# Masks on ScalarE without GpSimd's three small operations, and the first chunk's reciprocals spread by matmuls instead of copies and transposes

## The chip, the core and the metric

The kernel runs on one core of a Trainium2 chip. The metric is the device time of one execution in microseconds (us). Engines are named as in the profile: PE is TensorE (PEld its weight loads), DVE is VectorE, ACT is ScalarE, POOL is GpSimd, SP is SyncE, which issues the DMAs.

## What is computed

Attention over 4 batches of 8 heads, 576 rows, head size 64, in which each row keeps only its 32 largest scores; behind it two MLPs of 512 to 2048 to 512 over the 2304 rows.

```
scores = scale * q @ k.T
kth = 32nd largest score of the row
scores = where(scores >= kth, scores, -1e9); attn = softmax(scores)
x = attn @ v                                   # (2304, 512)
h = x @ w_in;  x = (h - tanh(h)) @ w_out       # first MLP
h = x @ w_in;  out = elu(h) @ w_out            # second MLP
```

## The kernel before

**Tiling.** The 2304 rows are cut into six chunks of 384 rows (CHUNKS). A chunk has four pairs of heads, a pair two groups, a group three tiles of 128 rows by 576 scores: 48 groups of three tiles in all, eight per chunk. Chunk 0's attention has nothing beside it but the preparation of the weights (a 64-bit format that `prepare` turns into two float parts: ACT at L186, L203 and L148, DVE at L189, POOL at L149). From then on the MLP steps of one chunk run on PE beside the attention of the next chunk, whose search for the 32 largest scores runs on DVE.

**The search.** `topk_steps` (L387) makes a chain of four rounds for each group. A round has a `find` for each tile (DVE's MAX8, the eight largest values left, into the tile `vm`) and a `drop` for each tile. In rounds 0 to 2 `drop` is DVE's MATCH_REPLACE8 (L420), which takes the eight values out of the working copy. In round 3 the eighth value of `vm` is the row's 32nd largest score, the threshold, and `drop` makes the masked exponentials `e`, in one of two ways. For the first `by_act` tiles of a group ACT does it with two activations over 128x576: a Prelu (L422) that sends everything below the threshold to a very large negative number and leaves the rest, then an Exp (L423) that also sums the row. The other tiles have had their Exp in round 1 (L410), and DVE multiplies them by the comparison with the threshold (L427, a scalar_tensor_tensor that reads `s` and `e`). MASK_ACT sets `by_act`: three tiles per group in chunk 0 (not in its last group, which is the hurried one), two in chunk 1, one in chunk 2, none later. These are 7, 8 and 8 groups, 23 in all.

ACT's two activations need two small columns per tile: `nk`, minus the threshold, as the bias of the Prelu, and `b2`, the threshold times SCALE plus `mb`, as the bias of the Exp (`mb` is minus SCALE times the row's largest score, from round 0). POOL makes them in three operations on 128x3, 128x2 or 128x1 (L412, L413, L414), after the last of the group's MAX8 that ACT's tiles need. POOL's queue also holds the low parts of all operands (L149: gate, keys, weights), the low part of the queries (L326), the clearing of halves of the query tiles (L294), `mb` (L408) and the row sums (L498).

**Norm and attend.** `transposed` (L433) turns `e` round with PE transposes (L448) and copies it to `ph` on ACT (L449). `norm` (L490) takes the reciprocals of the row sums (DVE, L501, a tile `r` of 128x6) and has to spread them from "one per row" to a tile `rs` of 128x384, in which the 64 partitions of a head hold that head's reciprocals along the columns. For units with one head, as in chunk 0, ACT copies each reciprocal 64 times into `rw` (L513, one copy of 128x192 for each head), PE transposes `rw` in three pieces (L519), and ACT copies the result to `rs` (L532). For units with two heads, as in chunk 1, PE multiplies the column of `r`, repeated 64 times by a stride of zero as the weights, with the identity (L523); each such fp32 product is two MATMUL instructions. `attend` (L451) multiplies with the values (L470). The last pair of chunk 0 ("hurried") is the hand-over: its result is what the first MLP step waits for.

**The order.** The program issues all this in ticks (L731 on), but the framework's planner sets the order of each engine's queue from the order of issue, the priorities and its own estimate of each operation's time (`schedule_with_timeline_sim=True`, L809). On the chip each queue runs strictly in that order. `vm` and `b2` have two buffers each, so a group's `vm` is written again by the group after next, once every reader of the old content is done.

Of the kernel before, what the change touches and what calls it, by code (L numbers as in the profile page):

```python
# [8 lines left out]
F32 = mybir.dt.float32  # L9
# [4 lines left out]
AF = mybir.ActivationFunctionType  # L14
ALU = mybir.AluOpType
# [3 lines left out]
P = 128  # L19
# [4 lines left out]
SCALE = 0.125  # L24
# [3 lines left out]
NF = DFF // P  # L28
FILL = -1.0e38

STEEP = 3.0e38


CHUNKS = [
# [72 lines left out]
def tile_topk_attention_two_mlps(  # L107
# [9 lines left out]
    nc = tc.nc  # L117

    def pool(name, bufs, space=None):
        kw = {} if space is None else {"space": space}  # L120
        return ctx.enter_context(tc.tile_pool(name=name, bufs=bufs, **kw))

    const = pool("const", 1)
    sb = pool("sb", 2)
# [32 lines left out]
    def bank(tag, name, bufs):  # L157
        if tag == "h":
            if "park" in pairs:
                turns.close()  # L160
                del pairs["park"]
                pairs["h"] = pool("ph", 1, PSUM)
            return pairs["h"].tile([P, 512], F32, tag=tag, name=name, bufs=bufs)
        return ps.tile([P, 512], F32, tag=tag, name=name, bufs=bufs)
# [68 lines left out]
    for ci, size in enumerate(SIZES):  # L233
        for p in range(NPAIR):
            row = []
            c0 = 0
            for b, q0, n in CHUNKS[ci]:
                for heads in ([[0], [1]] if n >= 256 else [[0, 1]]):
                    u = Unit()
# [18 lines left out]
            for us in cuts:  # L258
                g = Group()
# [11 lines left out]
    def hurried(u):  # L271

        return u.rush and u.last
# [64 lines left out]
    def segments(u, t):  # L338

        out = []  # L340
        for i, h in enumerate(u.heads):
            lo, hi = max(0, i * u.n - t * P), min(P, (i + 1) * u.n - t * P)
            if lo < hi:
                out.append((lo, hi, h, t * P + lo - i * u.n))
        return out
# [41 lines left out]
    def topk_steps(g, r):  # L387

        k = len(g.tiles)
        if r == 0:  # L390
            g.vm = sb.tile([P, 4, 2, 8], F32, tag="vm", name=f"vm{g.id}")
            g.mb = sb.tile([P, 4], F32, tag="mb", name=f"mb{g.id}")
            g.sum = sb.tile([P, 4], F32, tag="sum", name=f"sum{g.id}", bufs=8)
            g.w = [sb.tile([P, S], F32, tag="w3", name=f"w3{g.id}_{j}", bufs=W_BUFS) for j in range(k)]
        if r == 1:
            for u in g.units:
                u.e = [sb.tile([P, S], F32, tag="e", name=f"e{u.id}_{t}", bufs=E_BUFS) for t in range(u.k)]

        by_act = 0 if g.rush and hurried(g.units[-1]) else min(k, MASK_ACT[g.units[0].ci])
        if r == 3 and by_act:  # L400
            g.nk = sb.tile([P, 4], F32, tag="nk", name=f"nk{g.id}")
            g.b2 = sb.tile([P, 4], F32, tag="b2", name=f"b2{g.id}")

        def find(j):
            u, t = g.tiles[j]
            nc.vector.max(g.vm[:, j, min(r, 1)], u.s[t] if r == 0 else g.w[j])  # L406
            if r == 0 and j == k - 1:
                nc.gpsimd.tensor_scalar_mul(g.mb[:, :k], g.vm[:, :k, 0, 0], -SCALE)  # L408
            if r == 1 and j >= by_act:
                nc.scalar.activation(u.e[t], u.s[t], AF.Exp, bias=g.mb[:, j : j + 1], scale=SCALE)  # L410
            if r == 3 and j == by_act - 1:
                nc.gpsimd.tensor_scalar_mul(g.nk[:, :by_act], g.vm[:, :by_act, 1, 7], -1.0)  # L412
                nc.gpsimd.tensor_scalar_mul(g.b2[:, :by_act], g.vm[:, :by_act, 1, 7], SCALE)  # L413
                nc.gpsimd.tensor_add(g.b2[:, :by_act], g.b2[:, :by_act], g.mb[:, :by_act])  # L414

        def drop(j):
            u, t = g.tiles[j]
            v = g.vm[:, j, min(r, 1)]
            if r < 3:
                nc.vector.match_replace(g.w[j], v, u.s[t] if r == 0 else g.w[j], FILL)  # L420
            elif j < by_act:
                nc.scalar.activation(u.e[t], u.s[t], AF.Prelu, bias=g.nk[:, j : j + 1], alpha=STEEP)  # L422
                nc.scalar.activation(  # L423
                    u.e[t], u.e[t], AF.Exp, bias=g.b2[:, j : j + 1], scale=SCALE, accum_out=g.sum[:, j : j + 1]
                )
            else:
                nc.vector.scalar_tensor_tensor(  # L427
                    u.e[t], u.s[t], v[:, 7:8], u.e[t], op0=ALU.is_ge, op1=ALU.mult, accum_out=g.sum[:, j : j + 1]
                )

        return [lambda j=j, d=d: d(j) for d in (find, drop) for j in range(k)]

    def transposed(g, blk):  # L433
# [52 lines left out]
    def spread(u):  # L486

        return u.ci >= 2 and not quick(u)

    def norm(ci, p, u):  # L490

        r = sb.tile([P, 8], F32, tag="r", name=f"r{ci}_{p}")
        a, seen = {}, {}
        at = 0
        for v in pair_units[ci, p]:
            if id(v.g) not in seen:
                seen[id(v.g)] = at
                nc.gpsimd.tensor_scalar_add(r[:, at : at + len(v.g.tiles)], v.g.sum[:, : len(v.g.tiles)], 1e-9)  # L498
                at += len(v.g.tiles)
            a[v.id] = seen[id(v.g)] + v.j0  # L500
        nc.vector.reciprocal(r[:, :at], r[:, :at])  # L501
        if spread(u):
            u.at = a
            u.flat = dr.tile([at * P], F32, tag=f"rd{ci}_{p}", name=f"rd{ci}_{p}")
            nc.sync.dma_start(u.flat.rearrange("(t p) -> p t", p=P), r[:, :at])
            return
        rt = bank("at", f"rt{ci}_{p}", 3)
        for v in pair_units[ci, p]:
            if len(v.heads) == 1:
                h = v.heads[0]  # L510
                if h == 0:
                    wide = sb.tile([P, 3, 2, D], F32, tag="rw", name=f"rw{v.id}", bufs=1)
                nc.scalar.activation(  # L513
                    wide[:, : v.k, h], r[:, a[v.id] : a[v.id] + v.k].unsqueeze(2).to_broadcast([P, v.k, D]), copy
                )
                if h == 1:
                    for t in range(v.k):
                        c = v.c0 + t * P
                        nc.tensor.transpose(rt[:, c : c + P], wide[:, t].rearrange("p h d -> p (h d)"), ident)  # L519
                continue  # L520
            for t in range(v.k):
                for lo, hi, h, c in segments(v, t):
                    nc.tensor.matmul(  # L523
                        rt[h * D : h * D + D, v.c0 + c : v.c0 + c + hi - lo],
                        r[:, a[v.id] + t : a[v.id] + t + 1].to_broadcast([P, D]),
                        ident[:, lo:hi],
                        start=True,
                        stop=True,
                    )
        n = SIZES[ci]  # L530
        u.rs = sb.tile([P, NMAX], F32, tag="rs", name=f"rs{ci}_{p}", bufs=1)
        nc.scalar.activation(u.rs[:, :n], rt[:, :n], copy)  # L532
# [198 lines left out]
    for tick in range(FIRST_TICK, n_ticks):  # L731
# [10 lines left out]
        for u in units:  # L742
            if hurried(u) and tick == 4 * u.g.at + 4:
                for blk in range(NB):
                    transposed(u.g, blk)
                norm(u.ci, u.p, u)
                attend(u)
                finish_pair(u)
        at, r = divmod(tick, 4)
        chain = topk_steps(groups[at], r) if 0 <= at < len(groups) else []  # L750
        todo = [step_parts(i) for i in at_tick.get(tick, ())]
        cuts = [len(chain) * j // (2 * max(1, len(todo))) for j in range(2 * max(1, len(todo)) + 1)]
# [60 lines left out]
```

## Time and profile before

| | us |
|---|---|
| median of 3 runs | 1217.75 (1216.57 to 1219.38) |
| the profiled execution | 1221.19 |
| its span, first to last instruction | 1219.4 |
| PE busy | 1150.4 (94%) |
| DVE busy | 950.1 (78%) |
| ACT busy | 764.1 (63%) |
| POOL busy | 503.1 (41%) |

The shares are over the whole span and mix stages. Cut into 40 slices, DVE is over 90% busy in nearly all of the first third and falls off later, PE is at 60 to 70% in the first five slices and at 90% or more from the eighth on, and ACT is full in slices three to six. The chain of work that ended last is PE almost alone (58% of the span, MATMULs of lines L613 and L577) back to 465 us, and DVE's search before that. So the first 465 us are where something other than PE can set the time.

### The profile page before, as it was taken

The page shows a single profiled execution, that of the slowest core. Times are in us where ns is not written, and L with a number is a line of the kernel's source. Part 1 is how long each engine was busy: PE and PEld are TensorE (multiplying, and loading weights), DVE is VectorE, ACT ScalarE, POOL GpSimd, SP SyncE. Part 2 cuts the span into 40 slices and gives each one's busy share as a digit, 9 for nine tenths or more (in the row PEclk, how much of TensorE's full clock was granted, in tenths as well). Part 3 has the DMA queues.
Part 4 walks back from the last instruction along what each step waited for, and adds up shares of the span by engine and source line. Part 5 has one row for each costly group of instructions (what it writes and reads, how often), then busy time and mean ns, then how long its engine had stood idle before and what let it go on. Part 6 is the DMA issues. An engine that isn't in the chain of part 4 may idle for free.

```text
span 1219.4 us, 18848 instructions
## 1 busy us (share of the span) xinstructions
PE 1150.4 (94%) x6349; PEld 976.2 (80%) x6349; DVE 950.1 (78%) x1896; ACT 764.1 (63%) x1592; POOL 503.1 (41%) x557
## 2 busy tenths in 40 slices
PE   6477789998999999999999999999999999999998
PEld 3344478887887978898988988988988988898897
DVE  7899999998999999789888779898789996100111
ACT  4999978988975546474564666575555564432333
POOL 2345348666752323253524444434434413333221
PEclk9688899998999999999999999999999999999999
DMA  7999728984989985759886779988679875686572
GB/s 233 361 354 336 241 73 295 365 288 142 385 345 290 288 302 144 246 162 315 251 187 206 238 239 247 226 243 271 218 248 221 205 154 207 210 285 247 195 270 95
DMA packets 81328, 299.59 MB, mean 246 GB/s; under 512 B 18768, under 2 KB 36048, under 8 KB 51664
## 3 DMA queue, kind: packets, MB, share of 16 engines
q1 hardware_dynamic: 81232, 298.39, 76.8%
q8 instruction: 50, 0.82, 0.3%
q14 instruction: 46, 0.38, 0.1%
HBM read 252.97 MB, written 45.39 MB: 245 GB/s over the span
## 4 chain that ended last, share of the span: by engine, by line
PE 58%; ACT 2%; DVE 1%; POOL 0%; issue 0%; ACTq 0%; POOLq 0%; DVEq 0%
PE acc L613 24%; PE h L577 24%; PE av L470 3%; PE pt L448 3%; PE ps L383 2%; PE ps L384 2%; DVE vm L406 0%; ACT y L627 0%; DVE w L420 0%; ACT zh L632 0%; ACT e L410 0%; ACT ph L449 0%; ACT s L385 0%; POOL kk L149 0%; ACT t L583 0%
## 5 line engine op out<-in xcount | busy, mean ns | idle before, releaser
L149 POOL TENSOR_TENSOR gl<-g,gh 128x384 fp32r<-128x384 f32 x192 | 203.4, 1061 | 371.8 <-ACT gh L148 352.3
L406 DVE MAX8 vm<-w 128x8 f32<-128x576 f32 x432 | 315.8, 748 | 3.2
L613 PE MATMUL acc<-wt,gh 128*128 128x512 f32 x1002 | 267.2, 398 | 0.3 <-ACT gh L148 0.3
L420 DVE MATCH_REPLACE8 w<-vm,w 128x576 f32<-128x576 f32 x288 | 212.8, 740 | 0.0
L613 PEld LDWEIGHTS acc<-wt,gh 128*128 128x128 f32 x1002 | 183.7, 188 | 33.9 <-issue 2.7
L148 ACT ACTIVATE gh<-g 128x384 fp32r<-128x384 f32 x192 | 100.6, 526 | 83.8 <-DVE g L591 43.3
L591 DVE SCALAR_TENSOR_TENSOR g<-t,h 128x384 f32<-128x384 f32 x96 | 52.4, 545 | 127.8 <-ACT t L583 127.4
L577 PE MATMUL h<-zh,wt 128*128 128x384 f32 (+2 forms) x768 | 145.8, 326 | 2.4 <-ACT zh L632 1.2
L613 PE MATMUL acc<-wt,gl 128*128 128x512 f32 x501 | 146.4, 398 | 0.0
L577 PE MATMUL h<-xh,wt 128*128 128x384 f32 x664 | 140.0, 339 | 2.0 <-DVE g L591 1.2
L448 PE MATMUL pt<-ident,e 128*116 128x128 f32 (+1 forms) x720 | 117.8, 290 | 20.2 <-ACT e L423 8.3
L385 ACT ACTIVATE s<-ps 128x288 f32<-128x288 f32 (+1 forms) x272 | 106.8, 416 | 45.2 <-PE ps L384 36.6
L406 DVE MAX8 vm<-s 128x8 f32<-128x576 f32 x144 | 107.4, 751 | 34.6 <-ACT s L385 32.6
L577 PEld LDWEIGHTS h<-zh,wt 128*128 128x128 f32 x768 | 124.9, 190 | 8.8 <-ACT zh L632 2.4
L449 ACT ACTIVATE ph<-pt 116x384 f32<-116x384 f32 (+1 forms) x240 | 111.2, 500 | 30.0 <-PE pt L448 29.5
L448 PEld LDWEIGHTS pt<-ident,e 128*116 128x116 f32 (+1 forms) x720 | 90.4, 143 | 43.2 <-ACT e L423 11.4
L577 PEld LDWEIGHTS h<-xh,wt 128*128 128x128 f32 x664 | 116.2, 188 | 9.0 <-DVE g L591 1.5
L582 ACT ACTIVATE t<-h 128x384 f32<-128x384 f32 x96 | 46.7, 488 | 108.2 <-PE h L577 108.0
L613 PEld LDWEIGHTS acc<-wt,gl 128*128 128x128 f32 x501 | 92.1, 188 | 18.5
L420 DVE MATCH_REPLACE8 w<-vm,s 128x576 f32<-128x576 f32 x144 | 106.6, 741 | 0.0
L580 ACT ACTIVATE t<-h 128x384 f32<-128x384 f32 x96 | 47.0, 491 | 90.9 <-PE h L577 90.8
L596 DVE TENSOR_TENSOR g<-h,t 128x384 f32<-128x384 f32 x76 | 41.4, 546 | 72.0 <-ACT t L580 71.5
(82 smaller groups left out, 1958.3 us busy)
## 6 DMA issues: line engine op xcount, KB each, us to landing
wt<-w SPq DMA_DIRECT2D x167, 1024.0 KB, 6.0
wr<-in_w_dram SPq DMA_DIRECT2D x32, 1024.0 KB, 8.9
w<-wp SPq DMA_DIRECT2D x32, 1024.0 KB, 8.4
kraw<-in_kT_dram SPq DMA_DIRECT2D x96, 144.0 KB, 5.4
vraw<-in_vL_dram SPq DMA_DIRECT2D x64, 160.0 KB, 5.2
sd<-sp SPq DMA_DIRECT2D x24, 288.0 KB, 5.8
s<-sd SPq DMA_DIRECT2D x24, 288.0 KB, 8.9
qraw<-in_qT_dram SPq DMA_DIRECT2D x64, 96.0 KB, 5.6
```

What stands on the lines that cost most here:

```text
L148: nc.scalar.activation(hi, src, copy)
L149: return nc.gpsimd.tensor_sub(lo, src, f(hi))
L385: nc.scalar.activation(s[lo:hi, cs], pt[lo:hi, :HS], copy)
L406: nc.vector.max(g.vm[:, j, min(r, 1)], u.s[t] if r == 0 else g.w[j])
L420: nc.vector.match_replace(g.w[j], v, u.s[t] if r == 0 else g.w[j], FILL)
L448: nc.tensor.transpose(pt[:kn, j * P : j * P + P], v.e[t][:, k0 : k0 + kn], ident)
L449: nc.scalar.activation(g.ph[:kn, blk, :nq], pt[:kn, :nq], copy)
L577: nc.tensor.matmul(h[:, cs], wv[:, wi, kt], xs[:, kt, cs], start=(a == 0), stop=(a == len(jobs) - 1))
L580: nc.scalar.activation(t, h, AF.Tanh)
L582: nc.scalar.activation(t, h, AF.Relu, scale=-1.0)
L591: nc.vector.scalar_tensor_tensor(g, t, -1.0, h, op0=ALU.add, op1=ALU.max)
L613: nc.tensor.matmul(acc[ci, m][t], gx[:, t * P : t * P + P], wt[:, wi], start=(ft == 0 and k == 0), stop=(ft == NF - 1 and k == 2),)
```

## The change

Two edits. The mask's first activation now takes minus the score plus the threshold (scale -1, bias the threshold itself out of `vm`), so that what is kept is negative or zero; the Prelu multiplies that part by 2^-100 and leaves the positive part, which is to vanish; the Exp's scale is -SCALE times 2^100. `nk` is gone, and `b2` is one scalar_tensor_tensor on DVE. In `norm`, chunk 0 takes the way of the units with two heads.

```diff
-STEEP = 3.0e38
+FLAT = 2.0**-100
...
         if r == 3 and by_act:
-            g.nk = sb.tile([P, 4], F32, tag="nk", name=f"nk{g.id}")
             g.b2 = sb.tile([P, 4], F32, tag="b2", name=f"b2{g.id}")
...
             if r == 3 and j == by_act - 1:
-                nc.gpsimd.tensor_scalar_mul(g.nk[:, :by_act], g.vm[:, :by_act, 1, 7], -1.0)
-                nc.gpsimd.tensor_scalar_mul(g.b2[:, :by_act], g.vm[:, :by_act, 1, 7], SCALE)
-                nc.gpsimd.tensor_add(g.b2[:, :by_act], g.b2[:, :by_act], g.mb[:, :by_act])
+                nc.vector.scalar_tensor_tensor(
+                    g.b2[:, :by_act], g.vm[:, :by_act, 1, 7], SCALE, g.mb[:, :by_act], op0=ALU.mult, op1=ALU.add
+                )
...
             elif j < by_act:
-                nc.scalar.activation(u.e[t], u.s[t], AF.Prelu, bias=g.nk[:, j : j + 1], alpha=STEEP)
+                nc.scalar.activation(u.e[t], u.s[t], AF.Prelu, bias=v[:, 7:8], scale=-1.0, alpha=FLAT)
                 nc.scalar.activation(
-                    u.e[t], u.e[t], AF.Exp, bias=g.b2[:, j : j + 1], scale=SCALE, accum_out=g.sum[:, j : j + 1]
+                    u.e[t], u.e[t], AF.Exp, bias=g.b2[:, j : j + 1], scale=-SCALE / FLAT, accum_out=g.sum[:, j : j + 1]
                 )
...
         for v in pair_units[ci, p]:
-            if len(v.heads) == 1:
+            if ci and len(v.heads) == 1:
                 h = v.heads[0]
```

In the last hunk chunk 0's four pairs leave out eight copies (L513) and twelve transposes (L519) and go on to the loop at L521 with six products each; the quick pairs of chunks 2, 3 and 5 keep the copies.

## Rows read from the trace of the kernel before

**Rows 1.** Busy time by stage: PE, PEld, DVE, ACT, POOL, then clock, DMA share, GB/s
```profile
34.00:165.00 131.00, 97.38 (x394) 61.13 (x394) 127.78 (x255) 122.83 (x244) 55.93 (x71) 0.80 0.83 294
165.00:330.00 165.00, 154.62 (x927) 135.12 (x927) 155.61 (x283) 142.62 (x279) 113.34 (x104) 0.97 0.75 272
330.00:465.00 135.00, 132.23 (x777) 110.35 (x773) 133.51 (x276) 80.60 (x162) 47.80 (x69) 1.00 0.90 289
```

**Rows 2.** Timeline of PE: start, duration, what, in brackets its idle time and releaser
```profile
174.16 2.29 PE L577 MATMUL h<-xh,wp 128*128 128x384 f32 x8 [2.69 <-DVE g L596]
...
200.33 0.40 PE L383 MATMUL ps<-kk,qs 128*128 128x288 f32 x1 [2.25 <-ACT s L385]
...
368.47 1.66 PE L577 MATMUL h<-xh,wt 128*128 128x384 f32 x8 [1.18 <-DVE g L591]
...
465.22 1.66 PE L577 MATMUL h<-zh,wt 128*128 128x384 f32 x8 [0.76 <-DVE g L591]
```

**Rows 3.** Line L412 on POOL (min/median/max ns), and its main wait (us, times)
```profile
L412 POOL TENSOR_SCALAR nk<-vm x23: 213/224/1202, 36.7 to 475.1; 128x2 f32<-128x2 f32 x8, 128x1 f32<-128x1 f32 x8, 128x3 f32<-128x3 f32 x7
...
  DVE vm L406: 21.5, 11
```

**Rows 4.** Timelines of DVE, POOL and ACT around 195 us
```profile
191.18 0.74 DVE L406 MAX8 vm<-w 128x8 f32<-128x576 f32 x1
...
192.64 2.31 POOL L149 TENSOR_TENSOR kk<-kraw,kk 128x576 fp32r<-128x576 f32 x1
194.93 0.21 POOL L412 TENSOR_SCALAR nk<-vm 128x2 f32<-128x2 f32 x1
...
195.18 1.45 ACT L422 ACTIVATE e<-s,nk 128x576 f32<-128x576 f32 x2 [3.18 <-POOL nk L412]
```

**Rows 5.** Timeline of DVE: a small operation, and an operation behind the one it reads
```profile
62.43 0.18 DVE L501 RECIPROCAL r<-r 128x6 f32<-128x6 f32 x1
62.53 2.04 DVE L406 MAX8 vm<-w 128x8 f32<-128x576 f32 x3
...
82.67 0.74 DVE L420 MATCH_REPLACE8 w<-vm,s 128x576 f32<-128x576 f32 x1
83.44 0.76 DVE L406 MAX8 vm<-w 128x8 f32<-128x576 f32 x1
```

**Rows 6.** L427 from 165 us on, by line and by group; one of them, and POOL beside it
```profile
L427 DVE SCALAR_TENSOR_TENSOR e<-s,vm,e x23: 793/808/1816, 176.5 to 477.0; 128x576 f32<-128x576 f32 x23
...
L427 DVE SCALAR_TENSOR_TENSOR e<-s,vm,e 128x576 f32<-128x576 f32 x22 | 22.3, 1014 | 0.2
...
196.82 1.50 DVE L427 SCALAR_TENSOR_TENSOR e<-s,vm,e 128x576 f32<-128x576 f32 x1
...
195.31 2.40 POOL L149 TENSOR_TENSOR wp<-wf,wp 128x1024 fp32r<-128x1024 f32 x1
```

**Rows 7.** Timelines of DVE and POOL around 119 us
```profile
117.39 1.41 DVE L406 MAX8 vm<-w 128x8 f32<-128x576 f32 x2
...
118.16 2.39 POOL L149 TENSOR_TENSOR wp<-wf,wp 128x1024 fp32r<-128x1024 f32 x1
...
120.92 1.23 DVE L189 SCALAR_TENSOR_TENSOR wf<-wr 128x1024 uint32<-128x1024 uint32 x1 [1.27 <-POOL b L413]
```

**Rows 8.** Timelines of ACT and PE: the spreading of the reciprocals, both ways
```profile
155.98 0.35 ACT L513 ACTIVATE rw<-r 128x192 f32<-128x192 f32 x1
156.23 0.48 ACT L449 ACTIVATE ph<-pt 116x384 f32<-116x384 f32 x1
...
159.09 0.55 PE L519 MATMUL rt<-ident,rw 128*128 128x128 f32 x3
...
214.96 0.94 PE L523 MATMUL rt<-ident,r 128*64 128x128 f32 x16
```

**Rows 9.** Timelines of ACT and DVE around 40 us: the readers and the next writer of vm
```profile
38.41 2.10 ACT L422 ACTIVATE e<-s,nk 128x576 f32<-128x576 f32 x3
...
39.78 0.75 DVE L406 MAX8 vm<-s 128x8 f32<-128x576 f32 x1
```

## The prediction

> **What bounds the kernel now.** I read the busy time by stage first, because a share over the whole span mixes stages with different limits. From 34 to 165 us DVE is busy 127.78 of 131 us and ACT 122.83, while PE has a quarter of the time free; from 165 to 330 us PE (154.62 of 165) and DVE (155.61) run level; from 330 to 465 us DVE has 1.5 us of 135 free and PE 2.8 [rows 1]. So the search on DVE sets the length of the first stage, and it paces the next two together with PE. Then I read PE's timeline for its idle time, since the chain that ended last is PE almost alone from 465 us on, so that every gap ahead of that is carried to the end. Four gaps matter: 2.69 us at the hand-over, 2.25 us at 200 us, 1.18 us at 368 us and 0.76 us at 465 us [rows 2]. Three are released by a gate on DVE, and the one at 200 us by an ACT copy. What makes that copy late is in the timelines just before it: ACT stood 3.18 us before a Prelu for POOL's `nk`, which started at 194.93 behind a split of the keys of 2.31 us, although the MAX8 that it needed had started at 191.18 [rows 4]. This is the place at which POOL in the mask's path costs time.
>
> **The change, part by part.**
>
> *What leaves POOL.* 69 operations of about 0.2 us, and L412's waits for DVE, 21.5 us in 11 cases [rows 3]. No gap of PE in [rows 2] is released by POOL, so this is worth nothing by itself. What is behind it on POOL's queue, the low parts of gates, keys and weights, comes earlier or stays.
>
> *What leaves ACT's wait.* The Prelu now waits for the MAX8 alone. At 195 us that takes away up to 3.18 us on ACT, and the copy, and PE's products behind it, move up. PE gets back at most its own gap: -2.25, which I take whole, since a gate of ACT and not of DVE was last there. Ends: -3.2, if what is queued behind the wait on ACT gains as well, and 0, if DVE is late by then. Other waits for `nk` are followed by no gap of PE that ACT released; I count them as nothing, covered by the products that PE has queued.
>
> *What comes to DVE: its own time.* 23 scalar_tensor_tensors on a few columns. No row has one; the nearest is the reciprocal of 128x6, which takes 0.18 us, but the next operation starts 0.10 us after it [rows 5]. Each stands right behind the MAX8 that it reads. Such a neighbour costs more: a MAX8 that reads what the operation before it wrote started 0.77 us after it, where two independent ones are 1.41 - 0.76 = 0.65 us apart [rows 5, 7], so 0.12 on top. I take 0.10 + 0.11 = 0.21 each; ends 0.08 (no dependence cost, and shorter than the reciprocal) and 0.30 (0.18 + 0.12). In chunk 0 there are 7, on the engine that sets the stage: +1.5 (0.6 to 2.1). In chunk 1 there are 8, +1.7 on DVE, which has 165 - 155.61 = 9.4 us free there: nothing, and +1.7 if the cover is gone. In chunk 2, 7 of the 8 lie before 465 us, with DVE full and two of PE's gaps waiting for it: +1.5 (0.6 to 2.1).
>
> *What comes to DVE: waiting beside POOL.* The new operation reads two tiles of SBUF, `vm` and `mb`. The nearest row of that kind is the masks by DVE, L427, which reads `s` and `e`: median 0.81 us, but mean 1.01 and maximum 1.82, and the one at 196.82 took 1.50 us while a POOL subtraction that had started at 195.31 ran until 197.71 [rows 6]. So such an operation can be held until POOL's is over. The mean addition is 1.01 - 0.81 = 0.20 us. For 7 in chunk 0 that is +1.4; one place can be seen: the MAX8s end at 118.80 while POOL's subtraction runs until 120.55, 1.75 us more, but DVE is idle for 1.27 us just behind [rows 7], which takes back most of it. With the 3.2 us that DVE has free in the stage [rows 1], I take half: +0.7 (0 to 2.2). In chunk 2 POOL had mostly stood waiting at these places, as the 11 waits show [rows 3], so I take 0 (up to 7 times 0.20 = 1.4).
> The Trainium skill's page "SBUF — State Buffer", section "Who interferes with whom", says that a DVE instruction with two SBUF inputs contends with a GpSimd instruction that reads SBUF, and that whoever comes first keeps the shared port for the whole instruction. By that rule the small operation is blocked for whatever is left of a POOL operation, so it speaks against the change, and the row at 196.82 agrees with it; by the mean it would put 23 times 0.20 = 4.6 us on DVE, where I count 0.7.
>
> *The reader of `vm`.* ACT's Prelus now read `vm` themselves, so the group after next can write it only when they are done. In group 0 they end at 40.51, and the next writer started at 39.78 [rows 9]: 0.73 us of wait for DVE in the old order. The planner knows of it and has other MAX8s to put first: 0 (up to 0.7).
>
> *The reciprocals.* Eight copies leave ACT; each held it for 156.23 - 155.98 = 0.25 us [rows 8]. Six of them lie in the stage that DVE sets, where ACT has 8 us free of 131 [rows 1] but now and then keeps DVE waiting for scores: 6 times 0.25 = 1.5 us of ACT, of which I take -0.6 (0 to -1.5). Two lie at the hand-over among the copies that the products with the values wait for: -0.5. Against that, twelve products replace three transposes in each pair. The 16 of a later pair took 0.94 us for as many columns (8 of 128 and 8 of 64, or 12 of 128), the three transposes 0.55 [rows 8]: +0.4 at the hand-over on PE, nothing in the other pairs, where PE is free. Together at the hand-over -0.1 (-0.5 to +0.4).
>
> **Sum:** 1.5 + 0.7 + 1.5 - 2.25 - 0.6 - 0.1 = +0.75, say +0.8 us. The profiled execution took 1221.19 us, 3.4 above the median of the runs, so 1222.0 in its terms and 1218.5 against the median of 1217.75. A measurement of this kernel can tell some 0.2% (2.4 us) from no change, so this is no change.
>
> **Rivals.** *Faster: ACT is the one that is relieved.* The whole wait of 3.18 us is won and not only PE's gap, all six copies count (-1.5), the hand-over gains its 0.5, and the new operations cost their low end (14 times 0.08 = 1.1): -3.18 - 1.5 - 0.5 + 1.1 = -4.1, or 1213.7 us. For it: ACT is 94% busy in the first stage and the only engine that was seen to wait long for `nk` [rows 1, 4]. Against: the gaps of PE at 368 and 465 us are DVE's [rows 2], and a faster ACT doesn't move those. A new order by the planner could add to it: the gate behind the 2.69 us at the hand-over [rows 2] stands among MAX8s, and if it is put earlier, part of that is won too.
>
> *Slower: the wait for the port decides.* Each new operation is held behind POOL's subtraction in progress, on the engine that sets the time. With the mean of 0.20 on top of 0.21 everywhere that is 14 times 0.41 = 5.7 us before 465 us; in chunk 1 8 times 0.41 = 3.3 us use up a third of DVE's free time, and if the gate that PE needs behind 200 us is then late, the 2.25 us aren't won: 5.7 - 0.7 = +5.0, or 1222.8 us; with the 2.25 won, 1220.5. It decides from about 0.4 us each on: 14 times 0.4 = 5.6 against gains of 3. For it: [rows 6] and DVE's share in [rows 1]. Against: at most of these places POOL was idle, and the first stage has some slack. The rule of the page named above is this rival's mechanism.
>
> *No net effect because both happen* is the forecast itself; the `vm` wait (+0.7) changes nothing in it.
>
> **How the numbers follow.** Forecast (within 0.2%): 0.38. Faster: 0.34; slower: 0.28. Gains and costs are of one size, each hangs on one row that shows it once, and the planner may lay out the order anew, so neither side gets less. The range takes in both rivals' times and a part of the hand-over's 2.69 at the low end: 1212.5 to 1223.0; the forecast's own is the 0.2% to either side of the median, 1215.3 to 1220.2. It leaves out about 1 in 10 on each side, a new order that costs or gains more.
>
> **What would show it.** Right: no ACT wait before a Prelu of more than a few tenths; PE's gap near 200 us gone; the new DVE line with a median under 0.3 us and a few of more than 0.5 where POOL subtracts; the products behind the hand-over's gap, at 174.16 before [rows 2], one to two us later. Wrong: the new line's mean above 0.5 us (slower); DVE's idle time before 330 us grown, or a hand-over that starts earlier (faster); or a gap of several us at a place where neither edit acts, which would be the planner's order.

## The result and the profile after

After the change the kernel takes 1225.95 us (median of 4 runs, 1223.43 to 1226.79); the kernel before, on the same chip, 1217.16 (4 runs, 1216.42 to 1219.38). The ratio is 1.0066, 95% interval 1.0045 to 1.0086: 8.8 us slower by the medians, outside the predicted range.

The stages of after, as in [rows 1]:

```profile
34.00:165.00 131.00, 98.52 (x429) 63.08 (x428) 128.75 (x261) 120.33 (x234) 49.97 (x50) 0.82 0.83 296
165.00:330.00 165.00, 156.09 (x942) 136.32 (x940) 159.63 (x295) 145.94 (x283) 107.42 (x82) 0.97 0.80 278
330.00:465.00 135.00, 129.26 (x731) 107.69 (x730) 132.00 (x281) 76.07 (x155) 42.14 (x47) 0.99 0.87 273
```

POOL is busy some 6 us less in each stage. DVE has 4 us more from 165 to 330 us, and from 330 to 465 us PE does 46 instructions fewer. PE's larger gaps in after (timeline of PE, to be laid beside [rows 2]):

```profile
172.69 1.65 PE L576 MATMUL h<-xh,wp 128*128 128x384 f32 x8 [1.13 <-DVE g L595]
...
195.34 2.93 PE L576 MATMUL h<-xh,wp 128*128 128x384 f32 x8 [2.69 <-DVE g L595]
...
277.79 0.89 PE L447 MATMUL pt<-ident,e 128*116 128x128 f32 x3 [2.80 <-ACT s L385]
...
334.32 0.54 PE L447 MATMUL pt<-ident,e 128*116 128x128 f32 x3 [2.92 <-ACT ph L448]
...
472.69 1.67 PE L576 MATMUL h<-zh,wt 128*128 128x384 f32 x8 [1.76 <-DVE g L590]
```

The gap at 200 us that ACT's copy released is gone, and there are others at 195, 334 and 472 us. The one at 277 us is not new. The kernel before has it too, released by ACT as well, and [rows 2] leaves it out (timeline of PE, before):

```profile
277.74 0.61 PE L383 MATMUL ps<-kk,qs 128*128 128x288 f32 x1 [2.28 <-ACT s L385]
```

What stands behind two of the others is seen on DVE, POOL and ACT of after (timelines; the lines are from 190 and from 333 us):

```profile
190.75 3.40 DVE L189 SCALAR_TENSOR_TENSOR wf<-wr 128x1024 uint32<-128x1024 uint32 x1
194.08 0.75 DVE L405 MAX8 vm<-w 128x8 f32<-128x576 f32 x1
194.75 0.53 DVE L595 TENSOR_TENSOR g<-h,t 128x384 f32<-128x384 f32 x1
...
190.69 2.39 POOL L149 TENSOR_TENSOR wp<-wf,wp 128x1024 fp32r<-128x1024 f32 x1
...
332.83 1.06 ACT L148 ACTIVATE wp<-wf 128x1024 fp32r<-128x1024 f32 x1 [1.24 <-DVE wf L189]
333.79 0.85 ACT L448 ACTIVATE ph<-pt 116x384 f32<-116x384 f32 x2
```

At 195 us the gate (L595) that PE waits for stands on DVE's queue behind the joining of a weight, which itself was held beside POOL until 193.08, and behind a MAX8. At 334 us the copy that PE waits for stands on ACT's queue behind a split that waits for DVE. Neither is an operation that the change added: it is what the planner put in front of what.

The new operation in after, by its line (count, then min/median/max ns):

```profile
L411 DVE SCALAR_TENSOR_TENSOR b<-vm,mb x23: 136/152/1495, 36.8 to 474.5; 128x2 f32<-128x2 f32 x8, 128x1 f32<-128x1 f32 x8, 128x3 f32<-128x3 f32 x7
```

The longest case, on DVE, and POOL beside it (timelines of after):

```profile
36.81 1.50 DVE L411 SCALAR_TENSOR_TENSOR b<-vm,mb 128x3 f32<-128x3 f32 x1
...
35.93 4.70 POOL L149 TENSOR_TENSOR wp<-wf,wp 128x1024 fp32r<-128x1024 f32 x2 [0.97 <-ACT wp L148]
```

Its median is 0.15 us, but the one at 36.81 took ten times that, while POOL ran subtractions that had begun 0.88 us earlier. So after shows both suspects at once: operations held beside POOL, and a new order with gaps where neither edit acts. The experiments take them apart.

### The profile page after: what moved, and what is told of

It is laid out like the page before. It is cut to its first block, busy times and chain, and to the rows that moved or that the text cites. A ratio compares the mean times of both kernels' runs of the same rounds, so it can differ in the third digit from the quotient of the medians.

```text
span 1224.9 us, 18889 instructions
## 1 busy us (share of the span) xinstructions
PE 1154.6 (94%) x6385; PEld 980.3 (80%) x6385; DVE 956.6 (78%) x1919; ACT 763.7 (62%) x1584; POOL 486.5 (40%) x488
## 4 chain that ended last, share of the span: by engine, by line
PE 66%; DVE 16%; ACT 8%; DMA 5%; issue 3%; POOL 1%; SPq 1%; ACTq 0%; POOLq 0%; DVEq 0%
PE h L576 27%; PE acc L612 26%; DVE vm L405 6%; DVE w L419 5%; PE av L469 4%; PE pt L447 4%; DMA wr<-in_w_dram 2%; PE ps L383 2%; PE ps L384 2%; DVE wf L189 1%; DVE e L426 1%; DMA s<-sd 1%; ACT s L385 1%; ACT wr L203 1%; DMA w<-wp 1%
## 5 line engine op out<-in xcount | busy, mean ns | idle before, releaser
L612 PE MATMUL acc<-wt,gh 128*128 128x512 f32 x1002 | 266.7, 398 | 0.5 <-ACT gh L148 0.5
L612 PEld LDWEIGHTS acc<-wt,gh 128*128 128x128 f32 x1002 | 183.6, 188 | 36.3 <-issue 3.9
L612 PE MATMUL acc<-wt,gl 128*128 128x512 f32 x501 | 146.9, 398 | 0.0
L447 PE MATMUL pt<-ident,e 128*116 128x128 f32 (+1 forms) x720 | 115.3, 286 | 26.1 <-ACT e L422 11.7
L612 PEld LDWEIGHTS acc<-wt,gl 128*128 128x128 f32 x501 | 92.2, 188 | 18.5
L595 DVE TENSOR_TENSOR g<-h,t 128x384 f32<-128x384 f32 x76 | 41.4, 545 | 71.5 <-ACT t L579 71.1
```

What stands on the lines that cost most here:

```text
L447: nc.tensor.transpose(pt[:kn, j * P : j * P + P], v.e[t][:, k0 : k0 + kn], ident)
L612: nc.tensor.matmul(acc[ci, m][t], gx[:, t * P : t * P + P], wt[:, wi], start=(ft == 0 and k == 0), stop=(ft == NF - 1 and k == 2),)
```

## The experiments

Theory A: the new operations on DVE, held beside POOL, make the loss. Theory B: the new order makes it. Theory C: the reciprocals' edit makes it.

### Each part alone, a variant, and a neutral edit, the order left to the planner

The mask edit alone, which is the diff without its last hunk:

> The mask edit alone; the first chunk's reciprocals are spread as before, and the planner lays the order out for this program. Theory A (the 23 new operations on DVE, held behind POOL, set the loss: about 9.8 us of DVE in the profile after, 6 of it where DVE sets the time): nearly the whole loss is here, ratio to before 1.004 to 1.008. Theory B (the planner's new order, the search ahead of the MLP's gates, makes the loss, and the operations cost little): an order of its own again, so the ratio is not tied to that of the whole change; anything from 0.996 to 1.008, with gaps of PE at other places than after's 195, 334 and 472 us. Theory C (the reciprocals by six matmuls make the loss): 0.998 to 1.001.

Measured: 1234.62 us against 1216.87, ratio 1.0148 (1.0130 to 1.0166). A part of the change loses twice what the whole loses, which is beyond the ranges of A and B alike.

The reciprocals' edit alone, which is that last hunk:

```
-            if len(v.heads) == 1:
+            if ci and len(v.heads) == 1:
```

> The reciprocals' edit alone; the masks are as before. Theory A: no more than its own small terms, -0.6 to +0.4 us, ratio 0.9985 to 1.0005. Theory B: the planner lays the order anew for this program as well, so the ratio can leave 0.998 to 1.002 on either side although only 8 copies and 12 products differ. Theory C: 1.004 to 1.008.

Measured: 1226.52 us, 1.0083 (1.0069 to 1.0097). The two parts' losses together would be 0.023, the whole has 0.0066: with the order left to the planner the parts don't add. B's range takes this in, and the interval does not rule out C's.

Both edits, with a bias that reads one tensor of SBUF:

```
-                nc.vector.scalar_tensor_tensor(
-                    g.b2[:, :by_act], g.vm[:, :by_act, 1, 7], SCALE, g.mb[:, :by_act], op0=ALU.mult, op1=ALU.add
-                )
+                for i in range(by_act):
+                    nc.vector.tensor_scalar(
+                        g.b2[:, i : i + 1], g.vm[:, i, 1, 7:8], SCALE, g.mb[:, i : i + 1], op0=ALU.mult, op1=ALU.add
+                    )
```

> Both edits, but the new bias is made by one tensor_scalar for each tile, with mb as its scalar, so that each reads one tensor of SBUF and does not share the port with POOL: 69 operations in place of 23. Theory A: their median stays at 0.06 to 0.15 us each and none is held for over 0.3 us, so 5 to 6 us of the loss are gone: ratio to before 0.999 to 1.002. Theory B: the holds go as well, but the time follows the order that the planner makes: anything from 0.996 to 1.008.

Measured: 1221.20 us, 1.0043 (1.0027 to 1.0059); there are 45 of the new operations, not the 69 that this expectation and a later one count. Theory A's 0.999 to 1.002 is missed, and B allows nearly anything, so by itself this run settles nothing.

The kernel before with two lines swapped:

```
-                nc.gpsimd.tensor_scalar_mul(g.nk[:, :by_act], g.vm[:, :by_act, 1, 7], -1.0)
                 nc.gpsimd.tensor_scalar_mul(g.b2[:, :by_act], g.vm[:, :by_act, 1, 7], SCALE)
+                nc.gpsimd.tensor_scalar_mul(g.nk[:, :by_act], g.vm[:, :by_act, 1, 7], -1.0)
```

> The kernel before with two of POOL's three small operations in the other order in the code (b2 is scaled before nk is made); the same instructions, the same work. Theory A and theory C: no difference, ratio 0.999 to 1.001. Theory B: the planner lays the order anew from there on, and the time moves by 2 us or more, ratio below 0.998 or above 1.002.

Measured: 1223.66 us, 1.0060 (1.0047 to 1.0073). The work is the same; `nk` comes one small POOL operation later, some 0.2 us [rows 3], and the planner lays out the order again. It costs 7 us, almost what the change costs. Since leaving `nk` out altogether wins only 1.7 us in the old order (below), the 0.2 us can hardly be the cause; the swap was not run with the old order held. Two of its gaps (timeline of PE):

```profile
175.21 0.52 PE L383 MATMUL ps<-kk,qs 128*128 128x288 f32 x1 [3.67 <-ACT s L385]
...
198.66 1.19 PE L613 MATMUL acc<-wp,gl 128*128 128x512 f32 x3 [1.84 <-POOL gl L149]
```

### The same edits with the old order held

To measure the edits without a new order, each engine's instructions were chained in the order that they have in the kernel before. At the end of the tile function stands

```
+    for _e, _perm in _ord.items():
+        _mine = [i for i in tc.nc.cur_bb.bb.instructions if str(i.engine) == "EngineType." + _e and type(i).__name__ != "BassTilePoolBoundary"]
+        for _a, _b in zip(_perm, _perm[1:]):
+            tc.add_manual_dep(_mine[_b], _mine[_a].name, mybir.DependencyInfo(mybir.DependencyClass.NoSync, mybir.DependencyReason.DATA), reason="pin")
```

with a table of the order. The chain is of the kind that asks for no semaphore (`NoSync`). In the profiles, the kernels held in this way run what they share with the kernel before in its sequence on PE, DVE, ACT and POOL, by operation, tile and shape; the kernel after differs from it on all four. The new operation stands behind the MAX8s and the `mb` that it reads; in two groups of the second chunk POOL makes `mb` late, and it stands two instructions further back.

Both edits:

> Both edits, with the instructions of each engine held in the order that they have in the kernel before (the new operation behind the MAX8 and the mb that it reads, the twelve products in the place of the transposes). Theory B: the loss of after (8.7 us) is gone, since the order is the old one; what is left are the terms of the prediction: holds of the new operation of some 0.4 us each (7 in the first stage, 7 before 465 us in the third: up to +5.6) against up to -2.25 for the wait for nk at 195 us: ratio 0.997 to 1.003. Theory A (the new operations on DVE make the loss in whatever order): 1.005 to 1.008.

Measured: 1223.77 us against 1217.10, 1.0059 (1.0041 to 1.0077). Theory A's range holds here and B's does not: in the old order the change still costs 5 to 9 us.

The mask edit alone:

> The mask edit alone in the old order of every engine. Theory B: as both edits in the old order within 0.1%, 0.997 to 1.003, against 1.0148 when the planner lays out the order for it. Theory A: 1.005 or more.

Measured: 1220.11 us, 1.0027 (1.0017 to 1.0037): 3.3 us, where the planner's order made it 18. Neither theory's expectation is met in full: A's 1.005 is not reached, and B's "as both edits" (1.0059) is not either.

The reciprocals' edit alone:

> The reciprocals' edit alone in the old order of every engine, the eight copies left out and the twelve products in the place of the transposes. Theory B: no difference that can be told, 0.998 to 1.001 (the prediction has -0.7 us for it), against 1.0083 when the planner lays out the order. Theory C (the products cost it): 1.004 or more.

Measured: 1218.98 us, 1.0017 (1.0004 to 1.0030): 2 us, where the planner's order made it 10. The interval leaves out theory C's 1.004, but a gain it is not.

Both, with the bias that reads one tensor:

> Both edits in the old order, the bias made by a tensor_scalar for each tile that reads one tensor of SBUF. Its distance to both edits in the old order is the price of the wait for the port with the order held: by the holds of after (0.32 us each, 14 where DVE sets the time) 3 to 5 us less, ratio to before 0.994 to 0.999; if the holds are covered by DVE's free time, no difference to it (within 0.1%).

Measured: 1219.62 us, 1.0022 (1.0011 to 1.0032). The expected 0.994 to 0.999 is missed, but what counts is the distance: 1.0059 - 1.0022 = 0.0037, some 4.5 us, less than with the operation that reads two. The wait for the port has a price, and this is it in this order; if anything it is more, since the 45 operations take more time of their own than the 23 (below: 0.35 us for three against 0.08 for one).

One place shows how it comes about. The third of these operations in three kernels, each fence with DVE first and POOL behind it (timelines). Both edits, old order:

```profile
67.15 2.11 DVE L411 SCALAR_TENSOR_TENSOR b<-vm,mb 128x3 f32<-128x3 f32 x1
69.18 0.75 DVE L405 MAX8 vm<-w 128x8 f32<-128x576 f32 x1
...
66.89 2.35 POOL L149 TENSOR_TENSOR wp<-wf,wp 128x1024 fp32r<-128x1024 f32 x1 [7.18 <-ACT wp L148]
```

The mask edit alone, old order:

```profile
66.81 0.76 DVE L405 MAX8 vm<-w 128x8 f32<-128x576 f32 x1
67.60 0.16 DVE L411 SCALAR_TENSOR_TENSOR b<-vm,mb 128x3 f32<-128x3 f32 x1
67.68 0.75 DVE L405 MAX8 vm<-w 128x8 f32<-128x576 f32 x1
...
67.67 2.37 POOL L149 TENSOR_TENSOR wp<-wf,wp 128x1024 fp32r<-128x1024 f32 x1 [7.68 <-ACT wp L148]
```

The bias by one tensor, old order:

```profile
67.60 0.44 DVE L412 TENSOR_SCALAR b<-vm,mb 128x1 f32<-128x1 f32 x3
67.95 0.75 DVE L405 MAX8 vm<-w 128x8 f32<-128x576 f32 x1
...
67.44 2.37 POOL L149 TENSOR_TENSOR wp<-wf,wp 128x1024 fp32r<-128x1024 f32 x1 [7.25 <-ACT wp L148]
```

In the first, POOL's subtraction had started 0.26 us earlier and DVE's operation ended with it, within 0.02 us: 2.03 us until the next MAX8. In the second POOL started 0.07 us later than the operation, and DVE lost 0.08 us. In the third POOL had started 0.16 us earlier, and three operations that each read one tensor went by in 0.35 us all the same. So whether POOL starts 0.26 us ahead of the operation or 0.07 us behind it is worth 2 us on DVE.

The new operation of both edits in the old order, by its line:

```profile
L411 DVE SCALAR_TENSOR_TENSOR b<-vm,mb x23: 160/161/2361, 35.0 to 477.8; 128x2 f32<-128x2 f32 x8, 128x1 f32<-128x1 f32 x8, 128x3 f32<-128x3 f32 x7
```

and DVE's groups there from 34 to 480 us (busy us, mean ns of one, idle time before them):

```profile
L189 DVE SCALAR_TENSOR_TENSOR wf<-wr 128x1024 uint32<-128x1024 uint32 x22 | 28.9, 1317 | 2.6 <-issue 2.1 <-ACT wr L203 0.5
...
L411 DVE SCALAR_TENSOR_TENSOR b<-vm,mb 128x3 f32<-128x3 f32 x7 | 6.5, 929 | 0.5
L411 DVE SCALAR_TENSOR_TENSOR b<-vm,mb 128x2 f32<-128x2 f32 x8 | 4.4, 548 | 1.1 <-POOL mb L407 0.8
L411 DVE SCALAR_TENSOR_TENSOR b<-vm,mb 128x1 f32<-128x1 f32 x8 | 1.7, 215 | 0.6
```

The 7 of the first chunk (128x3) take 6.5 us; unheld they would take 7 times 0.16 = 1.1. In the mask edit alone, in the same order, the same 7 take 2.8 us:

```profile
L411 DVE SCALAR_TENSOR_TENSOR b<-vm,mb 128x3 f32<-128x3 f32 x7 | 2.8, 393 | 0.4
```

So how much is waited hangs on where POOL happens to stand, and a small shift changes it.

### The new order by itself, and the one part that may win

After's own order, with the bias that reads one tensor:

> The changed kernel in its own order of every engine, but the bias is made by a tensor_scalar for each tile that reads one tensor of SBUF (three in the place of each new operation). If the waits for POOL (8.4 us over the 23 operations in the profile after) make the loss of after, the 69 small ones cost 0.08 us each in their place (5.7 us in all, against 9.8) and 4 us are won: ratio to before 1.002 to 1.004, as in the old order (1.0022). If after's order itself makes the loss (the search ahead of the MLP's gates, PE's gaps at 195, 334 and 472 us), they stay: 1.005 to 1.008.

Measured: 1225.23 us against 1217.73, 1.0061 (1.0049 to 1.0074). After itself is at 1.0066. So in after's order the waits are worth nothing that can be told (the two intervals leave room for some 3 us), and the loss is there without them. Its gaps are those of after (timeline of PE):

```profile
195.04 2.75 PE L577 MATMUL h<-xh,wp 128*128 128x384 f32 x8 [2.69 <-DVE g L596]
...
334.62 0.54 PE L448 MATMUL pt<-ident,e 128*116 128x128 f32 x3 [2.69 <-ACT ph L449]
472.12 2.93 PE L577 MATMUL h<-zh,wt 128*128 128x384 f32 x8 [2.18 <-DVE g L591]
```

The kernel before again, for a second profile:

> The kernel before once more, for a second profile: the first one's own time (1221.19 us) lies above all timed runs. Both theories: a time of 1214 to 1220 us, and the difference to the first profile ahead of the first MLP product at 180.6 us, where the loads of the start decide, with the time behind it the same within 1.5 us (1038.8 us).

Measured: 1215.56 us, with a span of 1213.8, 5.6 less than in the first profile. Two lines of it (timelines of DVE and PE):

```profile
30.95 1.29 DVE L189 SCALAR_TENSOR_TENSOR wf<-sc,wr 128x512 uint32<-128x512 uint32 x2 [2.37 <-ACT wr L203]
...
170.21 2.35 PE L577 MATMUL h<-xh,wp 128*128 128x384 f32 x8 [2.69 <-DVE g L596]
```

The hand-over comes at 170.21 instead of 174.16 [rows 2]: 3.95 of the 5.6 us arise ahead of it, 2.27 of them before the weight at 30.95, whose line stood at 33.22 in the first profile, behind a wait of 3.56 us for ACT's part. Behind the hand-over 1.7 us remain, a little more than the 1.5 expected. So later profiles are laid beside this one, and mostly behind the hand-over. How far the MLP's second product (L613 here, L612 in after) has come is read by counting it (windows with that line alone: PE busy and count, PEld busy and count). The kernel before again:

```profile
165.00:330.00 165.00, 60.79 (x225) 40.01 (x225) 0.97 0.76 275
330.00:480.00 150.00, 63.67 (x243) 44.18 (x243) 1.00 0.83 277
```

After:

```profile
165.00:330.00 165.00, 60.03 (x222) 39.67 (x222) 0.97 0.80 278
330.00:480.00 150.00, 58.62 (x222) 40.45 (x223) 0.99 0.82 260
```

At 480 us after is 3 + 21 = 24 products behind. Against the first profile of before, whose hand-over came later than after's, it is 15 (459 against 444). PE, which has almost no idle time from there on, can't give them back.

Four kernels with both edits now stand side by side. In the old order they are at 1.0022 without the waits and at 1.0059 with them; in after's order at 1.0061 without and 1.0066 with them. Either of the two, the waits or the new order, costs some 0.004 by itself, and both together hardly more. Where each is paid can be read from the start of the first of these products (by line: count, min/median/max ns, first and last start). The kernel before again, both edits in the old order, the same with one tensor, after, and after's order with one tensor:

```profile
L613 PE MATMUL acc<-wp,gh x150: 388/396/503, 176.7 to 369.6; 128*128 128x512 f32 x150
L612 PE MATMUL acc<-wp,gh x150: 388/394/500, 183.1 to 375.4; 128*128 128x512 f32 x150
L613 PE MATMUL acc<-wp,gh x150: 388/394/502, 177.1 to 368.7; 128*128 128x512 f32 x150
L612 PE MATMUL acc<-wp,gh x150: 388/394/502, 177.7 to 374.0; 128*128 128x512 f32 x150
L613 PE MATMUL acc<-wp,gh x150: 388/394/502, 177.4 to 373.9; 128*128 128x512 f32 x150
```

The first of them starts at 180.6 us in the first profile of before. From there to the end of the span (1219.4, 1213.8, 1221.0, 1216.5, 1224.9 and 1224.1 us) it is 1038.8 and 1037.1 us in the two profiles of before, 1037.9 and 1039.4 in the old order, and 1047.2 and 1046.7 in after's. So in the old order the waits are paid ahead of the first product, at 183.1 us, and nothing is lost behind it. In after's order the first product is not late, and 8 to 10 us are lost behind it, where the gaps at 195, 334 and 472 us lie.

Only the part that spares `nk`; `b2` stays with POOL, the reciprocals are as before:

```
-                nc.gpsimd.tensor_scalar_mul(g.nk[:, :by_act], g.vm[:, :by_act, 1, 7], -1.0)
...
-                nc.scalar.activation(u.e[t], u.s[t], AF.Prelu, bias=g.nk[:, j : j + 1], alpha=STEEP)
+                nc.scalar.activation(u.e[t], u.s[t], AF.Prelu, bias=v[:, 7:8], scale=-1.0, alpha=FLAT)
...
-                    u.e[t], u.e[t], AF.Exp, bias=g.b2[:, j : j + 1], scale=SCALE, accum_out=g.sum[:, j : j + 1]
+                    u.e[t], u.e[t], AF.Exp, bias=g.b2[:, j : j + 1], scale=-SCALE / FLAT, accum_out=g.sum[:, j : j + 1]
```

In the old order:

> Of the change only the part that spares nk: the Prelu takes the MAX8's last column itself (scale -1), POOL makes b2 by its two operations as before, DVE gets nothing, the reciprocals are as before; old order of every engine. If the new operation on DVE is what costs in the old order (mask alone there: 1.0027), this has no loss, and what the prediction put down for the Prelu's wait at 195 us is won at most: ratio 0.997 to 1.0005. If it is the earlier Prelu that costs (ACT's order, vm held longer by its readers): 1.002 to 1.004.

Measured: 1216.00 us against 1217.73, 0.9986 (0.9975 to 0.9997). This is faster than the kernel before and than after, the only one of all that is. Against the mask edit in the old order (1.0027) it differs by where `b2` is made: 0.0041, about 5 us, for the operation on DVE.

The hand-over and the place at 195 us in this kernel (timelines of PE, then of POOL):

```profile
169.54 2.33 PE L575 MATMUL h<-xh,wp 128*128 128x384 f32 x8 [1.46 <-DVE g L594]
...
198.14 0.97 PE L611 MATMUL acc<-wp,gl 128*128 128x512 f32 x3 [2.35 <-POOL gl L149]
...
192.89 0.73 POOL L407 TENSOR_SCALAR mb<-vm 128x3 f32<-128x3 f32 x1
193.59 0.19 POOL L412 TENSOR_TENSOR b<-b,mb 128x2 f32<-128x2 f32 x1
193.75 2.39 POOL L149 TENSOR_TENSOR wp<-wf,wp 128x1024 fp32r<-128x1024 f32 x1
196.11 1.98 POOL L149 TENSOR_TENSOR gl<-g,gh 128x384 fp32r<-128x384 f32 x1
```

The hand-over's gap is 1.2 us shorter than the 2.69 before. The reciprocals' edit in the old order has 1.40 us there and is not faster, so this does not show where the 1.7 us come from. At 198 us PE's gap is as long as before (2.35 for 2.25 us) and has another owner: the low part of a gate, which stands on POOL behind a split of weights.

The same kernel with the planner's order:

> The same kernel with the order laid out by the planner. If a new order costs by itself, as the swap of two operations did (1.006), this is slower than before although it only leaves work out: 1.002 to 1.015. If the planner's order follows the work: 0.997 to 1.0005, as with the old order.

Measured: 1224.35 us, 1.0051 (1.0037 to 1.0065). It only leaves work out, and with the order that the planner makes for it, it is 8 us slower than with the old one.

### Which engine's order it is

The kernel that spares `nk`, with only one engine's list left in the table of the order, and the planner free on the others. DVE's:

> The kernel that only spares nk (0.9986 in the old order, 1.0051 in the planner's), with DVE's order alone held to the old one; the planner lays out the other engines around it (PE 1223 lines apart from the old order). If the order of search and gates on DVE makes the loss: 0.997 to 1.001. If the other engines' orders do: 1.004 to 1.010.

Measured: 1230.54 us against 1216.84, 1.0123 (1.0105 to 1.0142), more than either case of the expectation.

PE's:

> The same kernel with PE's order alone held to the old one (DVE 907 lines apart). If the order of PE's products makes the loss (which of the MLP's and the attention's products stand first): 0.997 to 1.001. If DVE's order against a given PE does: 1.004 to 1.010, with gaps of PE released by gates.

Measured: 1241.84 us, 1.0221 (1.0197 to 1.0244), again more than expected. Its first stage (busy time by stage):

```profile
34.00:165.00 131.00, 82.90 (x324) 53.12 (x323) 119.06 (x232) 113.25 (x217) 48.83 (x59) 0.77 0.79 289
```

DVE, busy 127.78 us here in before [rows 1] and 128.75 in after, has 119.06 of 131: with PE's old order held, the planner lets the search run dry.

ACT's:

> The same kernel with ACT's order alone held; with it the planner gives nearly the old order elsewhere as well (PE 159 lines apart, DVE 89, POOL 16). Whichever engine counts, this is nearly the old order: 0.997 to 1.001. A time of over 1.004 would say that the 159 lines on PE or the 89 on DVE hold what makes the loss.

Measured: 1216.81 us, 0.9999 (0.9987 to 1.0010). None of the three owns the loss: DVE's or PE's old order with the others laid out anew is worse than all new. Only ACT's brings the time back, and it pulls the others along: by the expectations it leaves PE 159 lines and DVE 89 from the old order, where DVE's leaves PE 1223 and PE's leaves DVE 907. POOL's order was not held alone.

The reciprocals' edit (`if ci and len(v.heads) == 1`) added to the kernel that spares `nk`, in the old order of all engines:

> The kernel that only spares nk together with the reciprocals' edit, old order of every engine: the whole change but for the new operation on DVE (b2 stays with POOL). If the reciprocals' edit costs some 2 us (1.0017 in the old order by itself): 0.9995 to 1.001. If that was chance and the prediction's -0.7 us holds: 0.997 to 0.999. If both edits in the old order (1.0059) cost by something that only the two together bring, and not by the waits of the new operation: 1.003 or more.

Measured: 1217.26 us, 1.0006 (0.9996 to 1.0015); against 0.9986 without the edit that is again 2 us and more. The expectation's first case holds. Where they go, no line of either profile shows; that stays open.

## Why the prediction was wrong

The forecast was no change; the time is 8.8 us more, past both rivals. Two of its steps failed, and either one alone takes the kernel from 1.0022 to about 1.006; a third had the wrong sign. By its steps:

- **The wait for the port** was mis-sized. The step took +0.7 us in the first stage and 0 in the third, by half the mean of 0.20 us and by POOL being idle at most of these places. In the old order the wait costs some 4.5 us, as the pair with one and two tensors shows, by the profiles all of it ahead of the first MLP product; the first chunk's 7 operations alone are 6.5 - 1.1 = 5.4 us longer than unheld. The mean of [rows 6] was too small for a short operation: it can be held for as long as POOL's, up to 2.36 us, wherever it falls into one. With its own time the operation on DVE was put at 1.5 + 0.7 + 1.5 = +3.7 us; with `b2` on DVE instead of POOL as the only difference it measured 5.0, and 0.0053 or 6.5 with the reciprocals' edit. The slower rival had the mechanism, and its 1220.5 to 1222.8 us fell 1 us short of the 1223.77 of the old order. The rule of the Trainium skill's page "SBUF — State Buffer" ("Who interferes with whom") agrees with the three timelines at 67 us, first come and all of the operation. That the 4.6 us on DVE that it gave with the mean of [rows 6] came so near to 4.5 is luck: the 23 operations waited 12.6 - 23 times 0.16 = 8.9 us in that profile, and part of it came back elsewhere (last section).
- **The planner's order** was put at nothing. The prediction kept the old order in its sum and gave a new one 1 in 10 on each side, as if it could as well win. Every order that the planner laid out anew on all engines was slower than the kernel before, and five of the six were slower than the same kernel in the old order, the first of them barely:

  | kernel | the planner's order | the old order | difference |
  |---|---|---|---|
  | both, one tensor | 1.0043 | 1.0022 | 0.0021 |
  | `nk` spared | 1.0051 | 0.9986 | 0.0065 |
  | two lines swapped | 1.0060 | 1 (before) | 0.0060 |
  | both edits (after) | 1.0066 | 1.0059 | 0.0007 |
  | reciprocals | 1.0083 | 1.0017 | 0.0066 |
  | mask | 1.0148 | 1.0027 | 0.0121 |

  The old order is not one among equals, and an edit of a few instructions gives it up. For after itself the difference can't be told from none: its order costs 8 to 10 us behind the first MLP product and spares the waits ahead of it. Even with the old order kept, the two edits cost 7.2 us where the sum had 0.8.
- **The reciprocals** (-0.7) cost 2.0 and 2.4 us in the two comparisons: the wrong sign, and an error of about 3 us. The cause is open.
- **The operation's own time** was right: 0.16 us, with the next one 0.08 us behind it, and 0.79 us behind the start of the MAX8 that it reads (66.81 and 67.60 above), where independent ones are 0.65 apart [rows 5, 7]: 0.08 + 0.14 = 0.22, where the step took 0.21. But the +1.5 us for chunk 2 was not seen to be paid: behind the first MLP product both edits in the old order are no slower than before (1037.9 against 1037.1 and 1038.8).
- **ACT's relay at 195 us** (-2.25) was not won where it was looked for. The wait for `nk` is gone, but in the old order the kernel that spares `nk` has the same gap for a low part of a gate on POOL; in after it is a gate on DVE. The prediction named the end 0 "if DVE is late by then" and should have looked at who was next on every queue. Sparing `nk` does win 1.7 us (0.4 to 3.0) in the old order, so the size came near by luck; where it is won is not shown. The list of PE's gaps also lacked the 2.28 us at 277.74, which stays in after (2.80).
- **The reader of `vm`** (0, up to 0.7) was right: both edits in the old order have one wait of DVE for a Prelu that still reads `vm`, 0.5 us.
- **What leaves POOL** was rightly put at nothing by itself as far as is seen: the one version that wins still makes `b2` there. Of its 1.7 us the part of POOL's 23 spared operations was not told apart.
- **The signs.** The gap of several us at a place where neither edit acts came, at 334 us; it was named as the sign of the planner's order. A hand-over that starts earlier (172.69 instead of 174.16) was named as a sign of a faster kernel and misled, since the one profile of before was late: the second has 170.21.

In the old order the parts add up within the interval: -1.7 (`nk` spared) + 5.0 (`b2` on DVE) + 2.0 (reciprocals) = +5.3 us, where both together measured +7.2 (5.0 to 9.4). In the planner's orders they don't: there the two edits alone sum to 27 us, and together they have 8.8.

Shown are: the price of a new order for five kernels, two of which add no work (the swap, and `nk` spared); the port's wait as a cost in the old order; and that after's order has its loss without the waits (1.0061 against 1.0022 in the old one). Not shown is which decision of the planner costs what: the gates behind weights at 195 us and the copy behind a split at 334 us were read, not undone.

## What to carry to other kernels

Where a planner lays out the order, time an edit twice, with its own order and with the old one held; the first says what you get, the second what the edit is worth, and a neutral edit says how good the old order is. Two causes that each suffice don't add: here taking away the waits helped in one order and not in the other. A small operation put on a full engine costs what it may wait for, not its own time: look at the longest operation beside it on the shared port, and give it one input from SBUF, or leave it where it is. A gap is won only if nothing else is due there a moment later.

## What the runs showed of the hardware

- Holding is decided by who starts first: POOL 0.07 us behind the operation, no wait; 0.26 us ahead of it, 1.95 us more. At 319.99 us in after POOL was 0.06 us ahead, and the operation took 1.40 us.
- A TENSOR_SCALAR with a scalar per partition and one tensor of SBUF runs beside a POOL subtraction unhindered: in the old order 20 of the 45 began while one ran, and all 45 took 185 to 216 ns.
- In the old order part of the holds is only moved: with the new operations, the joining of weights (L189 at 128x1024) falls to a mean of 1317 ns, shown above, from 1515 in the second profile of before:

```profile
L189 DVE SCALAR_TENSOR_TENSOR wf<-wr 128x1024 uint32<-128x1024 uint32 x22 | 33.3, 1515 | 3.4 <-issue 1.7 <-POOL nk L412 1.0 <-ACT wr L203 0.7
```

  These are 22 times 0.198 us, or 4.4 us. The mask edit alone in the old order has 1356 ns, and the old order with the operations that read one tensor has 1500. That the small operations waited in its place is the likely reading; in after's order the mean is 1528, and nothing comes back.
- Two executions of one program differed by 5.6 us, 3.95 of it ahead of the hand-over at 170 us. The one profile that a prediction starts from can be such a one.
